# Values of a unit as four 128x128 products instead of sixteen 64x64 ones, and layer 1 of each expert on fewer slots

## The chip, the cores and the metric

The kernel runs on one core of one Trainium2 chip. The time is that of one execution on the device in microseconds (us), and kernels are compared by the medians of several runs. Engines: TensorE (PE in the profile; PEld is its weight load), VectorE (DVE), ScalarE (ACT), GpSimd (POOL) and SyncE (SP), which issues DMA transfers, as POOL and ACT also do.

## The reference

Linear attention with a norm, then a mixture of experts with one expert per token; only tokens with a positive skip score are computed.

```python
# q, k, v: (8, 8, 576, 64)
kv  = np.einsum('bhsd,bhse->bhde', k, v)              # a 64x64 state per batch and head
out = np.einsum('bhsd,bhde->bhse', q, kv)
rms = np.sqrt(np.mean(out * out, axis=-1, keepdims=True) + 1e-06)
out = out / rms * g_norm
x   = out.transpose(0, 2, 1, 3).reshape(4608, 512)
# experts: w_gate (512, 8), w1 (8, 512, 1024), w2 (8, 1024, 512)
do_compute = x @ w_skip > 0
xc = x[do_compute]                                    # other rows of x pass unchanged
e_idx  = np.argmax(xc @ w_gate, axis=1)
gate_w = softmax(xc @ w_gate)[chosen expert]
for e in range(8):
    mask = e_idx == e
    y[mask] = gate_w[mask] * (np.maximum(xc[mask] @ w1[e], 0) @ w2[e])
out[do_compute] = xc + y
```

## The kernel before, in words

Everything is in fp32 on PE. The order of the instructions on each engine is written out by hand: what the program issues first runs first on that engine.

**Attention.** Eight batches with eight heads each; the heads are taken as two groups u of four, and the four are indexed by w and a. For each batch `state` forms k-transposed times v in three thirds of 24 64x64 products each (`sum_ps`, line 336). `state_t` transposes the result (347), `state_m` multiplies it by the gate and skip weights (358), so that each head's state gets 9 more columns on either end for the router's logits, and `state_s` moves a copy to the other half of the partitions (366). After each of these ScalarE copies the result from PSUM into the batch's tile `kvd` (342, 350, 360, 369). There are five such tiles, and before the change each holds two versions of the state: index 0 as formed, index 1 with the partition halves exchanged.

The queries go in 36 units of 256 tokens by four heads: four units per batch (32 "ordinary" units, two token halves i by two head groups u), and after each four batches two units for the tokens left over (`x8`, i is None). A loop over n issues for each unit:

- `turn(n + 1)`: the next unit's queries are transposed by four PE transposes (403), and ScalarE copies them to `qT` (406);
- `values(n)`: `qT` times the state, 73 columns per head (443), into a PSUM tile of two banks, of which there are two; ScalarE squares them (449). For i = 0 `turn_8` also transposes left-over queries (422);
- `norm(n - 1)`: VectorE multiplies the previous unit by its inverse root mean square (474), with `squares` (457) and `root` (464) ahead of it; GpSimd adds the logits (491 to 497) and multiplies by the norm's weight into `xb` (507), and each batch's `xb` is stored;
- parts of the next batches' state, one third or one of `state_t`, `state_m`, `state_s` at a step: batch b's six parts stand at steps n-6 to n-1 ahead of its first unit n;
- loads of k and v three batches ahead and of q two ahead, on SyncE's queue, with stores of `xb` between them.

Beside this run the ranking of the experts and the slot numbers (VectorE, in groups at n = 12, 22 and at the end). When the second group is ranked, the weights of the first expert are loaded, behind which later stores of `xb` queue.

**Experts.** Experts are taken in order of their token counts, r = 0 to 7. Each has `CAPS[r]` slots; tokens over that would go through a loop of further rounds (line 1316). The slots are cut into pieces of 128, 64 and 32 (`plan_of`), and each piece's rows are gathered from `out` by an indirect DMA on GpSimd's queue (925), transposed (935) and copied to `xt`. For r = 0 both layers are direct products (`layer_1`, `layer_2`). From r = 1 on, `fast_1` forms layer 1 by Strassen's scheme, seven block products in place of eight, with half of the slots, `end // 2`, as the moving width (1033), sums on VectorE (975, 981, 1037) and copies on ScalarE (1043); it is 56 products of that width per expert. `fast_2` does the same for layer 2's first two pieces, and the rest of the pieces are direct products (965). In `fast_1` the next expert's tokens are transposed near the end, which needs their gathers. `result` (1166) adds the gated output to the gathered rows on VectorE and scatters them to `out` on GpSimd's queue (1175); the gathers of the next expert but one stand behind these scatters.

The widths of layer 1 and the pieces both follow from `CAPS`:

```python
    CAPS = (352, 352, 320, 288, 288, 288, 256, 256)
...
                todo = pieces[r]
                end = todo[-1][0] + todo[-1][1]
```

Of the kernel before, what the change touches and what calls it, by code (L numbers as in the profile page):

```python
# [8 lines left out]
FP32 = mybir.dt.float32  # L9
# [3 lines left out]
ALU = mybir.AluOpType  # L13
# [4 lines left out]
def kernel(  # L18
# [43 lines left out]
    nc = tc.nc  # L62
# [16 lines left out]
    PK = 2 * KD  # L79

    KVD = 5
    CAPS = (352, 352, 320, 288, 288, 288, 256, 256)
    CK = CAP // 128
    NCOL = E * CK
    ROUNDS = N // CAP
# [170 lines left out]


    kinds = {}
    for r, cap in enumerate(CAPS):
        off = cap // P * P  # L260
        for m in (64, 32):
            if cap - off >= m:
                kinds.setdefault((off % P, m), []).append((r, off))
                off += m
        assert off == cap
# [21 lines left out]
    gate_k = keep.tile([P, NT, 3], BF16)  # L287

    srow = keep.tile([P, NCOL], FP32)
    nc.vector.memset(srow[:, :], 0.0)  # L290

    top = keep.tile([P, E], FP32)
    nc.vector.tensor_copy(out=top[:, :], in_=ebase[:, :])
# [17 lines left out]

    kvds = []
    for i in range(KVD):
        kvds.append(kvd_pool.tile([P, 2, 2, PK], FP32, name=f"kvd{i}"))

    sum_all = ps_kv.tile([P, 2, 512], FP32, name="sum_ps")
    sum_ps = sum_all[:, :, 0:2 * D].rearrange("p a (u d) -> p a u d", u=2)
    sw_ps = g_ps[:, 0:2 * PK]
    kvT_ps = g_ps[:, 0:2 * P].rearrange("p (u x) -> p u x", u=2)
    lg_ps = g_ps[:, 2 * PK:2 * PK + 4 * G].rearrange("p (u a g) -> p u a g", u=2, a=2)  # L320

    def ends_of(x):

# [4 lines left out]
    def state(b, third):  # L328

        kt, vt = kts[b], vts[b]  # L330
        for i in range(6 * third, 6 * third + 6):
            u, c = divmod(i, C)
            for w in range(2):
                for a in range(2):
                    r = slice(a * 64, (a + 1) * 64)
                    nc.tensor.matmul(  # L336
                        out=sum_ps[w * 64:(w + 1) * 64, a, u, :],
                        lhsT=kt[r, 2 * u + w, c, :], rhs=vt[r, 2 * u + w, c, :],
                        start=(c == 0), stop=(c == C - 1), skip_group_check=True)
        if third < 2:  # L340
            return
        nc.scalar.copy(
            out=kvds[b % KVD][:, 0, :, G:G + 2 * D].rearrange("p u (a d) -> p a u d", a=2), in_=sum_ps)

    def state_t(b):
        for u in range(2):
            nc.tensor.transpose(out=kvT_ps[:, u, :], in_=kvds[b % KVD][:, 0, u, G:G + 2 * D],
                                identity=ident[:, :])
        kvT = att_pool.tile([P, 2, P], FP32, tag="kvT", name="kvT", bufs=1)
        nc.scalar.copy(out=kvT[:, :, :], in_=kvT_ps)  # L350
        kvTs[b] = kvT

    def state_m(b):
        kvT = kvTs.pop(b)
        for u in range(2):
            for w in range(2):
                r = slice(w * 64, (w + 1) * 64)
                nc.tensor.matmul(out=lg_ps[r, u, :, :], lhsT=kvT[:, u, r], rhs=gw_b[:, u, :, w, :],
                                 start=True, stop=True, skip_group_check=True)
        nc.scalar.copy(out=ends_of(kvds[b % KVD][:, 0, :, :]), in_=lg_ps)  # L360

    def state_s(b):

        for w in range(2):
            r, o = slice(w * 64, (w + 1) * 64), slice((1 - w) * 64, (2 - w) * 64)
            nc.tensor.matmul(out=sw_ps[o, :], lhsT=ident[r, r],  # L366
                             rhs=kvds[b % KVD][r, 0, :, :].rearrange("p u k -> p (u k)"),
                             start=True, stop=True, skip_group_check=True)
        nc.scalar.copy(out=kvds[b % KVD][:, 1, :, :].rearrange("p u k -> p (u k)"), in_=sw_ps)


    units = []
# [54 lines left out]
    def values(n):  # L427
        _, b, i, u = units[n]
        qT = qTs.pop(n)

        ps = sum_all if n >= THIRD and (n - THIRD) % 3 == 0 else \
            ps_o.tile([P, 2, 512], FP32, tag="o", name="o_ps")

        done = turn_8(b, u, ps) if i == 0 else None
        for w in range(2):
            for a in range(2):
                cols = slice(a * KD, (a + 1) * KD)
                for hf in range(2):
                    for r in range(2):
                        rows, to = slice(r * 64, (r + 1) * 64), slice(hf * 64, (hf + 1) * 64)  # L440
                        kvd = kvds[(b if i is not None else 4 * b + 2 * hf + r) % KVD]
                        x, y = (a, hf) if i is not None else (hf, a)
                        nc.tensor.matmul(  # L443
                            out=ps[to, r, w * PK + a * KD:w * PK + (a + 1) * KD],
                            lhsT=qT[rows, w, x, y * 64:(y + 1) * 64],
                            rhs=kvd[rows, w ^ r, u, cols],
                            start=True, stop=True, skip_group_check=True)
        sq = att_pool.tile([P, 2, 2, 2 * D], FP32, tag="sq", name="sq", bufs=2)
        nc.scalar.activation(out=sq[:, :, :, :], in_=heads(ps, G, G + 2 * D), func=ACT.Square)  # L449
        if done:  # L450
            done()
        ops[n] = (ps, sq)
# [27 lines left out]
    def finish(n, xl):  # L480
# [12 lines left out]
        if u == 1:  # L493
            del halves[nq]
            nc.gpsimd.tensor_tensor(out=lp[:, 0, :, :, :], in0=lp[:, 0, :, :, :],
                                    in1=lp[:, 1, :, :, :], op=ALU.add)
            nc.gpsimd.tensor_tensor(out=lgs[g][:, t0:t0 + 2, :], in0=lp[:, 0, :, 0, :],
                                    in1=lp[:, 0, :, 1, :], op=ALU.add)
        if i is None:
            if u == 0:  # L500
                xbs[b, i] = xb_pool.tile([P, 2, DM], FP32, tag="x8", name="x8", bufs=1)
# [1 line left out]
        else:  # L503
# [2 lines left out]
            xb = xbs[b, 0][:, i, :, :]  # L506
        late.append(lambda: nc.gpsimd.tensor_tensor(  # L507
            out=xb[:, :, 4 * u * D:(4 * u + 4) * D].rearrange("p r (w x) -> p r w x", w=2),
            in0=xl[:, :, :, G:G + 2 * D],
            in1=g_b[:, :, :].rearrange("p a d -> p (a d)").unsqueeze(1).unsqueeze(1)  # L510
                .to_broadcast([P, 2, 2, 2 * D]), op=ALU.mult))
        if n == NU - 2:
# [316 lines left out]
    with tc.tile_pool(name="wpool_b", bufs=1, reuse_waits="tile") as wpool_b, \  # L829
# [69 lines left out]


        def plan_of(r):
            pieces = [(c * P, P, r * CK + c) for c in range(CAPS[r] // P)]
            i = 0
            for (_, m), rs in kinds.items():
                for j, (r_, off) in enumerate(rs):
                    if r_ == r:
                        pieces.append((off, m, i + j))
                i += len(rs)
            return pieces
# [34 lines left out]
        def new_xt():  # L944
            return ffn.tile([P, DC, CAP], FP32, tag="xt", name="xt")

        def new_ht():
            return ffn.tile([P, FC, CAP], FP32, tag="ht", name="ht")

        def layer_1(r, xt, ht, cols, fs):  # L950
            for f in fs:
# [241 lines left out]
                for piece in pieces[r]:  # L1193
                    gather_piece(xgs[r], piece, src, asrc)

        def experts(pieces, srcs, xt, ht, yps0, tables, group):

            for r in range(E):
                load_ahead(r)
                if r:  # L1200
                    gather_all(r + 1, pieces, *srcs)
                todo = pieces[r]
                end = todo[-1][0] + todo[-1][1]
                new = {}

                def enter(some):
# [16 lines left out]
                    fast_1(r, xt, ht, end // 2, w2_sums(r), lambda: enter(more[0:1]))  # L1223
                    enter(more[1:])
                if more:
                    n = (more[-1][0] + more[-1][1]) // 2
                    beside = x_sums(r + 1, new["xt"], n) + (w1_sums(r + 1) if r else [])
                if r == 0:
                    for piece in todo:
# [12 lines left out]
                del w_sb[r]  # L1242
                if more:
                    xt, ht = new["xt"], new_ht()

        def rounds():

# [24 lines left out]
        assert plan[0][0] == first  # L1272
        plan[0] = plan[0][1:]
        xt0, ht0 = new_xt(), new_ht()
        expert_in(xg0, xt0, first)
        drain(choose(LAST))
        bv = columns(0, NE, colid_i, row_k, 2, gat_pool, NE)
# [19 lines left out]
        def first_tables(layer, tables):  # L1297
# [8 lines left out]
            agate = slot_pool.tile([P, NRES], FP32, tag="agate", name="agate")  # L1306
            nc.vector.tensor_copy(out=agate[:, :], in_=again_of(gate))
            return (tables[0], gate), (tables[1], agate)
        experts(plan, (src, asrc), xt0, ht0, yps0, (rows, arows), "first")

        order.__exit__(None, None, None)

# [3 lines left out]
        with tc.For_i(1, n_rounds, 1):  # L1316
            nc.vector.tensor_single_scalar(out=colid[:, :], in_=colid[:, :], scalar=CK, op=ALU.add)
            nc.vector.tensor_single_scalar(out=number_f[:, :], in_=number_f[:, :],
                                           scalar=float(CAP), op=ALU.add)
            nc.vector.memset(srow[:, :], 0.0)  # L1320
            add_pieces(srow[:, :], place_all(colid, row_k, 2), 2)

            left = slot_pool.tile([P, NCOL], FP32, tag="left", name="left")
            nc.vector.tensor_tensor(
                out=left[:, :].rearrange("p (r c) -> p r c", c=CK),
                in0=number_f[:, :].unsqueeze(1).to_broadcast([P, E, CK]),
                in1=caps[:, :].unsqueeze(2).to_broadcast([P, E, CK]), op=ALU.is_ge)
            nc.vector.tensor_tensor(out=srow[:, :], in0=srow[:, :], in1=left[:, :], op=ALU.mult)
            rows, src = slot_rows(slice(0, NCOL), slot_pool, "")
            for r in range(2):  # L1330
                gather_all(r, whole, src, None)
            gate = slot_gates(colid)
            xt0 = new_xt()
            for piece in whole[0]:
                expert_in(xg0, xt0, piece)
            experts(whole, (src, None), xt0, new_ht(), None, ((rows, gate), None), "more")


# [26 lines left out]
```

## Time and profile before

| | |
|---|---|
| median of 3 runs | 428.54 us (427.44 to 429.47) |
| the profiled execution | 427.44 us |
| its span, first to last instruction | 425.5 us |
| granted PE clock, mean | 0.92 |
| PE busy | 364.6 us (86%), 4601 matmul records |
| VectorE / ScalarE / GpSimd busy | 249.8 / 135.5 / 118.9 us |
| moved by DMA | 81.79 MB, 192 GB/s on average |
| first unit's values end | 19.2 us |
| first tokens of the experts transposed | 143.3 us |
| passes r = 1 to 7 begin | 199.3, 234.3, 264.0, 293.6, 324.2, 354.0, about 387 us |

A line of the profile's list gives start, duration, engine, line of the kernel, operation, the tiles and shapes, and how many alike; in brackets is how long the engine had been idle before it, and what ended that. "issue" there means that the profile shows nothing that the engine waited for. PE's matmuls are pipelined, so their rate is read from start to start and not from a row's own duration. An fp32 matmul appears as two matmul records, each with its weight load; a PE transpose as one.

### The profile page before, as it was taken

To read this page: it belongs to the slowest core of one execution; us is meant where nothing else is said; L and a number is where in the kernel's file an instruction comes from. 1 tells how busy PE (TensorE), PEld (TensorE's weight loads), DVE (VectorE), ACT (ScalarE), POOL (GpSimd) and SP (SyncE) were. 2 spreads that over 40 slices of the span, in tenths; PEclk is the share of its full clock that TensorE was granted. 3 is DMA by queue.
4 is the path that set the end of the run, shared out by engine and by line. 5 is a ranking of instruction groups with operands and counts; after the bars stand their busy time and mean duration, and the time that the engine had idled before them with its cause. 6 is when DMAs were issued, how large, how long until landed. Compare 5 with 4: busy or idle time off the path is not lost.

```text
span 425.5 us, 11081 instructions
## 1 busy us (share of the span) xinstructions
PE 364.6 (86%) x4601; PEld 309.6 (73%) x4601; DVE 249.8 (59%) x619; ACT 135.5 (32%) x360; POOL 118.9 (28%) x184
## 2 busy tenths in 40 slices
PE   7868775957876597999999999999999999989970
PEld 4556554746755484966987997998988988979960
DVE  3123353865887775154674765766766776858620
ACT  1344463445354230120340350240430430422300
POOL 2033454663456807012201221121121203101010
PEclk9589898879696698899999999999999999999995
DMA  8999989594769597052740733743752672501000
GB/s 302 390 390 385 326 233 373 169 298 168 211 229 347 140 295 261 10 219 66 236 176 36 250 102 156 245 118 153 246 193 77 237 241 79 205 27 50 2 27 20
DMA packets 31293, 81.79 MB, mean 192 GB/s; under 512 B 1850, under 2 KB 1858, under 8 KB 31236
## 3 DMA queue, kind: packets, MB, share of 16 engines
q1 hardware_dynamic: 26688, 66.59, 45.8%
q0 software_dynamic: 4528, 14.41, 10.5%
q8 instruction: 38, 0.62, 0.6%
q14 instruction: 19, 0.16, 0.1%
q10 hardware_dynamic: 20, 0.02, 0.0%
HBM read 66.80 MB, written 14.48 MB: 191 GB/s over the span
## 4 chain that ended last, share of the span: by engine, by line
PE 67%; issue 12%; DMA 11%; DVE 3%; ACT 2%; POOL 2%; SPq 0%; DVEq 0%; POOLq 0%; ACTq 0%
PE bank L1033 37%; PE bank L965 7%; PE bank L954 6%; PE sum_ps L336 5%; PE o_ps L443 4%; DMA out_dram<-xb 4%; DMA v<-in_v_dram 3%; PE q_ps L403 3%; DMA xg<-out_dram,src 2%; PE bank L935 2%; DVE xl L474 2%; DMA k<-in_k_dram 1%; DMA xg<-out_dram,asrc 1%; PE g_ps L366 1%; ACT qT L406 1%
## 5 line engine op out<-in xcount | busy, mean ns | idle before, releaser
L1033 PE MATMUL bank<-xt,w 128*128 128x144 f32 (+3 forms) x336 | 56.5, 291 | 0.3 <-DVE bank L1037 0.3
L1043 ACT COPY p<-bank 128x144 f32<-128x144 f32 (+4 forms) x70 | 20.9, 299 | 105.8 <-PE bank L1033 91.7
L1033 PEld LDWEIGHTS bank<-xt,w 128*128 128x128 f32 x336 | 47.8, 190 | 2.2 <-DVE bank L1037 1.5
L1037 DVE TENSOR_TENSOR bank<-bank,p 128x144 f32<-128x144 f32 (+4 forms) x70 | 23.8, 340 | 39.6 <-PE bank L1033 37.5
L336 PE MATMUL sum_ps<-v,k 64*64 64x64 f32 x1152 | 29.6, 248 | 13.5 <-issue 11.5
L1175 POOL DMA_INDIRECT out_dram<-xg,rows x16 | 16.2, 1011 | 79.6 <-DVE xg L1172 79.0
L507 POOL TENSOR_TENSOR xb<-xl,g_b 128x512 f32<-128x512 f32 x32 | 38.1, 1191 | 1.0 <-DMA out_dram<-xb 0.8
L336 PEld LDWEIGHTS sum_ps<-v,k 64*64 64x64 f32 x1152 | 26.4, 160 | 15.9 <-issue 15.3
L1033 PE MATMUL bank<-xs,s 128*128 128x144 f32 (+3 forms) x224 | 37.4, 292 | 0.0
L965 PE MATMUL bank<-w,ht 128*32 128x128 f32 (+2 forms) x448 | 36.6, 322 | 0.0
L443 PE MATMUL o_ps<-kvd,qT 64*64 64x73 f32 x960 | 27.7, 252 | 10.3 <-issue 6.2
L443 PEld LDWEIGHTS o_ps<-kvd,qT 64*64 64x64 f32 x960 | 22.0, 152 | 17.8 <-issue 12.3
L457 DVE TENSOR_REDUCE rs<-sq 128x8 f32<-128x512 f32 x36 | 24.5, 679 | 15.5 <-ACT sq L449 15.5
L1033 PEld LDWEIGHTS bank<-xs,s 128*128 128x128 f32 x224 | 31.6, 190 | 1.0 <-ACT p L1043 0.3
L925 POOL DMA_INDIRECT xg<-out_dram,src x15 | 15.9, 1063 | 55.7 <-PE bank L1033 36.3
L1175 POOL DMA_INDIRECT out_dram<-xg,arows x8 | 9.0, 1129 | 78.1 <-DVE xg L1172 77.8
L965 PEld LDWEIGHTS bank<-w,ht 128*32 128x32 f32 (+2 forms) x448 | 20.4, 121 | 13.6 <-issue 10.9
L406 ACT COPY qT<-q_ps 128x512 f32<-128x512 f32 x32 | 18.8, 587 | 32.5 <-PE q_ps L403 32.3
L491 POOL TENSOR_TENSOR lp<-xl 128x36 f32<-128x36 f32 x36 | 9.2, 255 | 71.3 <-DVE xl L474 69.4
L471 DVE RECIPROCAL rs<-rs 128x8 f32<-128x8 f32 x36 | 7.2, 200 | 36.8 <-ACT rs L464 36.2
L474 DVE TENSOR_TENSOR xl<-o_ps,rs 128x584 f32<-128x584 f32 x33 | 25.3, 767 | 4.0
L1033 PE MATMUL bank<-w,ht 128*128 128x256 f32 x112 | 27.1, 385 | 0.0
(196 smaller groups left out, 709.3 us busy)
## 6 DMA issues: line engine op xcount, KB each, us to landing
w<-in_moe_w_dram SPq DMA_DIRECT2D x16, 2048.0 KB, 10.7
q<-in_q_dram SPq DMA_DIRECT2D x8, 1152.0 KB, 12.9
k<-in_k_dram SPq DMA_DIRECT2D x7, 1152.0 KB, 12.2
v<-in_v_dram SPq DMA_DIRECT2D x7, 1152.0 KB, 15.1
out_dram<-xb SPq DMA_DIRECT2D x8, 512.0 KB, 4.6
out_dram<-xb POOLq DMA_DIRECT2D x8, 512.0 KB, 7.3
k<-in_k_dram SPq DMA_DIRECT2D x2, 576.0 KB, 4.1
v<-in_v_dram SPq DMA_DIRECT2D x2, 576.0 KB, 7.4
```

The source lines that it names most:

```text
L336: nc.tensor.matmul(out=sum_ps[w * 64:(w + 1) * 64, a, u, :], lhsT=kt[r, 2 * u + w, c, :], rhs=vt[r, 2 * u + w, c, :], start=(c == 0), stop ...
L406: nc.scalar.copy(out=qT[:, :, :, :].rearrange("p w a t -> p (w a t)"), in_=ps[:, :, :, :, :].rearrange("p w a h t -> p (w a h t)"))
L443: nc.tensor.matmul(out=ps[to, r, w * PK + a * KD:w * PK + (a + 1) * KD], lhsT=qT[rows, w, x, y * 64:(y + 1) * 64], rhs=kvd[rows, w ^ r, u, ...
L457: nc.vector.tensor_reduce(out=rs[:, :, :], in_=sq[:, :, :, :].rearrange("p x y (a d) -> p x (y a) d", a=2), axis=AX.X, op=ALU.add)
L474: nc.vector.tensor_tensor(out=xl[:, :, :, :].rearrange("p x y (a k) -> p x (y a) k", a=2), in0=ps[:, :, 0:2 * PK].rearrange("p x (h k) -> ...
L507: late.append(lambda: nc.gpsimd.tensor_tensor(out=xb[:, :, 4 * u * D:(4 * u + 4) * D].rearrange("p r (w x) -> p r w x", w=2), in0=xl[:, :, ...
L954: nc.tensor.matmul(out=hps[:, cols], lhsT=w_sb[r][0][:, dc, f * P:(f + 1) * P], rhs=xt[:, dc, cols], start=(dc == 0), stop=(dc == DC - 1))
L965: nc.tensor.matmul(out=yps[q * m:(q + 1) * m, 0:n], lhsT=ht[:, f, off:off + m], rhs=w_sb[r][1][:, f, q * n:(q + 1) * n], start=(f == 0), s ...
L1033: nc.tensor.matmul(out=out, lhsT=lhsT(i), rhs=rhs(i), start=start and i == 0, stop=i == k - 1, skip_group_check=True)
L1037: nc.vector.tensor_tensor(out=to, in0=x, in1=y, op=ALU.add)
L1043: nc.scalar.copy(out=t, in_=x)
L1175: ins = nc.gpsimd.indirect_dma_start(out=cut_rows(m)[:, :], out_offset=bass.IndirectOffsetOnAxis(ap=rows[:, col:col + 1], axis=0), in_=x, ...
```

## The change

Two things change.

1. For ordinary units the state tile `kvd` gets a second index and twice the room: for each copy w and each half r of the partitions it holds the state in one block and zeros in the other. A unit's sixteen products of 64x64 by 73 columns become four products of 128x128 by two pieces of 73 columns, in which one weight tile covers two heads' rows and the zeros keep them apart. The results of a unit lie in another order in PSUM, and the readers follow. `state_t` becomes four matmuls against halves of the identity in place of two transposes, `state_m` two matmuls in place of four, and each of ScalarE's three copies into `kvd` becomes two on half of the partitions. At the start the zeros are written, two memsets per tile, those of the first tile on VectorE and the others on GpSimd. The left-over units keep 64x64 products.

2. `CAPS` is smaller: 344, 336, 320, 280, 272, 264, 256, 256. `ROOMS` rounds it up to multiples of 32, which gives the former capacities, and the pieces, gathers and layer 2 go by `ROOMS`. Layer 1 runs on `CAPS[r]` columns. The columns of `ht` between the two are set to zero by GpSimd (`blank`), and slots over the capacity get row numbers out of range from the initial value of `srow`, which takes three small VectorE operations in place of a memset.

```diff
-    CAPS = (352, 352, 320, 288, 288, 288, 256, 256)
+    CAPS = (344, 336, 320, 280, 272, 264, 256, 256)
+    ROOMS = tuple(-(-cap // 32) * 32 for cap in CAPS)
...
-    nc.vector.memset(srow[:, :], 0.0)
+    beyond = setup.tile([P, CK], FP32)
+    nc.vector.tensor_single_scalar(out=beyond[:, :], in_=number_f[:, :], scalar=float(CAP), op=ALU.add)
+    nc.vector.tensor_tensor(
+        out=srow[:, :].rearrange("p (r c) -> p r c", c=CK),
+        in0=beyond[:, :].unsqueeze(1).to_broadcast([P, E, CK]),
+        in1=caps[:, :].unsqueeze(2).to_broadcast([P, E, CK]), op=ALU.is_ge)
+    nc.vector.tensor_single_scalar(out=srow[:, :], in_=srow[:, :], scalar=float(RSPACE), op=ALU.mult)
...
-        kvds.append(kvd_pool.tile([P, 2, 2, PK], FP32, name=f"kvd{i}"))
+        t = kvd_pool.tile([P, 2, 2, 2, PK], FP32, name=f"kvd{i}")
+        for r in range(2):
+            (nc.vector if i < 1 else nc.gpsimd).memset(t[r * 64:(r + 1) * 64, :, :, 1 - r, :], 0.0)
+        kvds.append(t)
+
+    def own(b, w):
+
+        return kvds[b % KVD][w * 64:(w + 1) * 64, :, w, w, :]
...
-        nc.scalar.copy(
-            out=kvds[b % KVD][:, 0, :, G:G + 2 * D].rearrange("p u (a d) -> p a u d", a=2), in_=sum_ps)
+        for w in range(2):
+            nc.scalar.copy(out=own(b, w)[:, :, G:G + 2 * D].rearrange("p u (a d) -> p a u d", a=2),
+                           in_=sum_ps[w * 64:(w + 1) * 64, :, :, :])
 
     def state_t(b):
         for u in range(2):
-            nc.tensor.transpose(out=kvT_ps[:, u, :], in_=kvds[b % KVD][:, 0, u, G:G + 2 * D],
-                                identity=ident[:, :])
+            for w in range(2):
+                r = slice(w * 64, (w + 1) * 64)
+                nc.tensor.matmul(out=kvT_ps[:, u, r], lhsT=kvds[b % KVD][:, u, w, w, G:G + 2 * D],
+                                 rhs=ident[:, r], start=True, stop=True)
...
         for u in range(2):
-            for w in range(2):
-                r = slice(w * 64, (w + 1) * 64)
-                nc.tensor.matmul(out=lg_ps[r, u, :, :], lhsT=kvT[:, u, r], rhs=gw_b[:, u, :, w, :],
-                                 start=True, stop=True, skip_group_check=True)
-        nc.scalar.copy(out=ends_of(kvds[b % KVD][:, 0, :, :]), in_=lg_ps)
+            nc.tensor.matmul(out=lg_ps[:, u, :, :, :], lhsT=kvT[:, u, :], rhs=gw_b[:, u, :, :, :],
+                             start=True, stop=True)
+        for w in range(2):
+            nc.scalar.copy(out=ends_of(own(b, w)), in_=lg_ps[w * 64:(w + 1) * 64, :, :, w, :])
...
+                if i is not None:
+                    nc.tensor.matmul(
+                        out=ps[:, w, 0:2 * PK].rearrange("p (r k) -> p r k", r=2)[:, :, cols],
+                        lhsT=qT[:, w, a, :], rhs=kvds[b % KVD][:, u, w, :, cols],
+                        start=True, stop=True, skip_group_check=True)
+                    continue
                 for hf in range(2):
                     for r in range(2):
...
-            pieces = [(c * P, P, r * CK + c) for c in range(CAPS[r] // P)]
+            pieces = [(c * P, P, r * CK + c) for c in range(ROOMS[r] // P)]
...
+        def blank(ht, r):
+            if CAPS[r] < ROOMS[r]:
+                nc.gpsimd.memset(ht[:, :, CAPS[r]:ROOMS[r]], 0.0)
...
-                end = todo[-1][0] + todo[-1][1]
+                end = widths[r]
...
-                    n = (more[-1][0] + more[-1][1]) // 2
+                    n = widths[r + 1] // 2
...
                     xt, ht = new["xt"], new_ht()
+                    if yps0 is not None:
+                        blank(ht, r + 1)
```

## The prediction

> **What bounds the kernel now.** Times are us from the start of the profiled execution: 427.44 us, 1.9 of them outside its span of 425.5; the median of the runs is 428.54. I read the busy table by stages, then TensorE's (PE's) waits up to 127, then its timeline.
>
> ```profile
> 19.20:101.80 82.60, 58.05 (x1686) 47.37 (x1686) 40.53 (x82) 37.62 (x94) 37.94 (x67) 0.88 0.91 311
> 101.80:127.10 25.30, 21.03 (x569) 17.32 (x569) 20.43 (x48) 14.58 (x37) 13.28 (x24) 0.87 0.58 178
> 127.10:143.30 16.20, 7.64 (x193) 6.29 (x193) 12.32 (x28) 6.63 (x16) 11.36 (x20) 0.75 0.81 272
> ...
> 354.00:385.00 31.00, 29.50 (x191) 27.02 (x192) 22.65 (x54) 8.44 (x25) 5.26 (x5) 1.00 0.32 104
> ```
>
> Columns: length; busy time of PE, PE's weight loads, VectorE (DVE), ScalarE (ACT), GpSimd (POOL); clock; DMA share; GB/s. No engine is full before 143, and nothing but PE is full after 199.
>
> ```profile
> PE sum_ps L336 <- issue: 11.5, 6, 3.5
> PE o_ps L443 <- issue: 6.2, 5, 2.2
> PE g_ps L358 <- issue: 4.8, 1, 4.8
> PE o_ps L443 <- DVE xl L474: 3.1, 4, 1.8
> ...
> PE sum_ps L336 <- DMA v<-in_v_dram: 1.0, 1, 1.0
> ```
>
> PE mostly waits for nothing the profile shows ("issue"), hardly for data. One such stop, inside a product whose operands are ready:
>
> ```profile
> 54.93 0.34 PE L443 MATMUL o_ps<-kvd,qT 64*64 64x73 f32 x4
> ...
> 57.49 0.73 PE L443 MATMUL o_ps<-kvd,qT 64*64 64x73 f32 x28 [2.22 <-issue]
> ```
>
> Counting PE's records (a weight load and a matmul each count one; an fp32 matmul makes two of both), the stops come before numbers 696, 951, 1206, 1462, 1716, 1972, 2227, 2482: 256 apart but for a few lost records. Each ends 1.2 to 1.5 us after a 16 KB packet of queue q8 lands, and PE makes 9,202 records for q8's 38 packets:
>
> ```profile
> q8 instruction: 38, 0.62, 0.6%
> ```
>
> So PE runs out of instructions there. Releases are 5.9, 6.5, 6.2, 7.7 and 6.6 us apart (38.91 to 71.71), mean 6.6: a refill's round trip under the loads. There are 13 stops up to 127: 23.0 us, 21.55 of them before 101.8. The trace's clock record adds half-speed stretches after long gaps (26.1-29.5, 46.6-50.0, 70.5-77.3, 90.9-97.8), with 15.8 us of PE work; 32 value products take 0.67 us at full and 1.18 at half clock, so about 6.8 us is lost there. Work at full clock up to 101.8 is 58.05 - 6.8 = 51.3.
>
> **Part 1, values as four 128x128 products.** PE's price is start to start in dense rows:
>
> ```profile
> 206.01 0.76 PE L1033 MATMUL bank<-xs,s 128*128 128x176 f32 x4
> 206.61 0.76 PE L1033 MATMUL bank<-xt,s 128*128 128x176 f32 x4
> ...
> 278.42 0.65 PE L1033 MATMUL bank<-xt,s 128*128 128x144 f32 x4
> 278.91 0.65 PE L1033 MATMUL bank<-xt,w 128*128 128x144 f32 x4
> ```
>
> Four take 0.60 at 176 columns, 0.49 at 144: 149 and 123 ns each (112 at 128, and 111.5 at 3 columns: a floor). Eight at 146 columns: 1.00 us. Before, from the start of one group to the start of the next at full clock, the transposes of a unit take 0.58 (33.01 to 33.59) and its values 0.56 to 0.67 (52.73 to 53.29, 33.59 to 34.26), mean 0.62. After, the transposes take 0.49, as they do where another 128-row group follows (83.90 to 84.39), the values 1.00, and 0.05 more because a 64x64 group follows half of them: 1.54, +0.34 per ordinary unit. The moving operand lies in two pieces of 73; no row here has that. If it cost like 176 columns, the unit would take +0.53; I take the 144-column row, the nearer in width.
>
> The Trainium skill, TensorEngine Tiling (Array Packing), Theoretical Speedup, gives 64x64 tiles up to 4x where both dimensions are small, and so speaks against the change: by the full 4x, an estimate, a unit would go from 0.62 to 2.48 and 27 units would cost 50 us, where the rows above make it 27 x 0.34 = 9.
>
> In state_t two transposes (0.28 to 0.35 to the next group) become four matmuls, eight records at the floor, 0.89; in state_m 0.35 becomes four records, 0.45. Together +0.68 per batch. state_s issues what it did.
>
> Stage to 101.8 (19 ordinary units, 5 batches' state): +6.5 + 3.4 = +9.9 of PE work. Records fall from 3,383 by 19 x 48, plus 5 x 4, to 2,491: 9.7 refills, not 13.2. Work per refill rises from 51.3 / 13.2 = 3.9 us to 61.2 / 9.7 = 6.3, against a round trip of 6.6. The work is uneven: of a batch's four steps, three hold 96 records of state sums each and run at 5.7 us per 256 records, the one with state_t is far slower. Stops remain where the dense part meets a refill, so I take 0.8 us per refill: 8 us instead of 21.55, -13.5. Ends: 0 us (-21.5) and 1.65 each as now (16 left, -5.5). Clock: short stops leave it up, -5.5 (ends 0 and -6.8). Waits for xl (1.2 here): -1.0, since PE comes later. Sum -10.1.
>
> By the Trainium skill, Runtime: NRT & Kernel Launch, Instruction fetch mechanics, refills of 256 instructions are mostly hidden; then nothing would be saved and the part would cost its +9.9. The 256 agrees with the trace; "hidden" does not (23.0 us of stops).
>
> 101.8 to 127: one refill stop (1.42), VectorE 20.4 of 25.3 with the ranking. 8 x 0.34 + 2 x 0.68 = +4.1; stop -0.7; xl wait (1.82) -1.3; the wait for state_s's copy (0.99) +0.4, there being two copies: +2.5.
>
> Start (half clock): VectorE's three small operations for srow (+0.4) and two memsets of 64x584 (between 0.12, the 128x72 memset, and 0.77, the 584-wide multiply; 0.5 each) let state_t begin at 13.4, not 12.54: +0.85; state_t +1.15, state_m +0.34, values of unit 0 +0.75; 0.93 is covered by the wait for v at 20.1: +2.2. Ends +0.5 and +4.
>
> 127 to 143: the end hangs on POOL and on stores behind 4 MB of weights (POOL's multiply at 136.87 waits for one). Values grow 4 x 0.34 or twice that at half clock; PE's own waits there (0.49, 1.38) cover most: +0.7. Ends 0 and +3.
>
> What I cost at nothing: ScalarE gets three more copies per batch (0.38 + 0.19 + 0.40): 8 us in all. It is 46% busy to 101.8 and the copies stand a step ahead of their readers; if its qT copy came late for them, up to 0.8 per batch. POOL's eight memsets of kvd (0.6 each by its 64x512 row, 0.51) run at 2 to 7 us, where it is idle to 20; the store of zeros behind them has no reader before 134. SyncE's queue keeps its order, and no transfer is added.
>
> **Part 2, layer 1.** Pieces, gathers and layer 2 stay, since the rooms are the old capacities. The inputs give 339, 333, 318, 275, 270, 264, 255 and 211 tokens by rank, so no second round runs; one expert fills its 264 slots exactly, and a chip that counted one token more would run the loop (0.01, among the slower). Passes 1, 3, 4, 5 shrink by 8, 4, 8, 12 columns in 112 records, pass 0 by 8 in 64; at 0.83 ns a column: 0.75, 0.37, 0.75, 1.1, 0.43 = 3.4. Passes 3 to 5 then meet the gathers:
>
> ```profile
> 311.33 0.95 POOL L925 DMA_INDIRECT xg<-out_dram,asrc  x1 [0.30 <-issue]
> ...
> 314.71 0.30 PE L935 MATMUL bank<-ident,xg 128*128 128x128 f32 x1 [0.52 <-DMA xg<-out_dram,asrc]
> ...
> 340.63 0.97 POOL L925 DMA_INDIRECT xg<-out_dram,src  x1 [0.30 <-issue]
> ...
> 344.23 0.63 PE L935 MATMUL bank<-ident,xg 128*128 128x128 f32 x4
> ```
>
> Tokens arrive 3.4 to 3.7 us after issue: pass 4 waits already, passes 5 and 3 (issue 280.87, need 284.25) have no slack, and the gathers follow the earlier pass's stores, not layer 1. So passes 0 and 1 pay (the latter has 2 us of slack) and 0.1 of the rest: -1.3. Ends -3.4 (gathers move along) and 0 (140 priced as 144, 168 as 176). The blanks (five POOL memsets, about 0.25 each by its small adds) stand between stores and gathers, where POOL waits 6 to 8 us; without that cover they would delay each gather by 0.25.
>
> **Sum:** -10.1 + 2.5 + 2.2 + 0.7 - 1.3 = -6.0; 427.4 - 6.0 = 421.4, said as 421. My base lies 1.1 below the median, less than the 0.5% (2.1 us) that a measurement can tell from no change.
>
> **Rivals.** (a) Refills stay as costly: denser loads stretch the round trip, each of 9.7 stops keeps 1.65 us and the half clock stays. Then +9.9 - 5.5 + 4.1 + 2.2 + 0.7 - 1.3 = +10: 437. For it: DMA share is 0.91 in that stage and rises if it shortens. Against: more work per refill. It decides where 9.7 stops eat what is gained: 9.9 - 1.0 + 4.1 = 13.0 of added work against 21.55 - 9.7 s, so from s = 0.9 us, or 1.4 if the clock mends by 5.5.
> (b) Refills hide entirely, clock full: -21.5 - 6.8 + 9.9 - 1.0 = -19.4, rest +4: 412. For it: 6.3 against 6.6. Against: round trips up to 7.7, and one stop of 4.77.
> (c) Another pace setter (loads, VectorE's chain) keeps the stage at 82.6: +2.5 + 2.2 + 0.7 - 1.3 = +4: 431. For it: DMA 0.91. Against: after 21 PE never waits for a load, and VectorE is at 49%.
> (d) The slots change nothing in time, since every pass meets its gathers: 1.3 higher, 423; a variant of each case, as is the full 3.4 (419).
>
> **Numbers.** Forecast 0.52, (a) 0.15, (b) 0.20, (c) 0.13. Forecast alone: 415 to 428. The bounds of the unknown costs (values up to 0.19 x 27 = 5 more, the start, the refills between 0 and 16, the gathers) carry it to 411 and 433; that leaves out about 0.11 of (a) and 0.06 of (b). Faster by 0.5% (below 426.4): 0.45 of the forecast, (b), and 0.04 of (c): 0.69. Within: 0.06 + 0.06 = 0.12. Slower: the rest, 0.19.
>
> **What would show it.** Right: value rows of x8 at about 1.0 us; "issue" before 102 falls to about 8; clock near 1 in 20-100; unit 22's values at about 94; the transposes into xt wait 0.3 to 1 us in passes 3 to 5. Wrong: stops above 1.4 us per refill, eight value records at 1.2 us or more, new PE waits for ACT's kvd copies, or a load that PE waits for.

## The result: 743.91 us, a second round of all experts

The changed kernel takes 743.91 us (median of 4 runs, 741.94 to 746.34) where the kernel before takes 427.99 in the runs beside it: a ratio of 1.7389, 95% interval 1.7296 to 1.7482. The forecast was 421. In all that follows, medians are over all runs and ratios over those in the faster of two states in which an execution can fall, so the two can differ a little.

The profiled execution took 741.94 us, with a span of 740.2. Its busy table in two stretches, up to the values of unit 22 and after the first round's last full products (columns as in the prediction: length; busy time of PE, weight loads, VectorE, ScalarE, GpSimd; granted clock; DMA share; GB/s):

```profile
19.20:86.10 66.90, 62.90 (x1253) 56.31 (x1252) 42.30 (x82) 44.94 (x112) 37.39 (x67) 0.99 1.01 362
...
391.00:740.00 349.00, 323.04 (x1572) 260.16 (x1570) 166.67 (x376) 78.03 (x193) 51.41 (x50) 0.96 0.32 98
```

The second line is new as a whole: the kernel before ends at 425.5. PE is busy for 323 us of it, almost nine tenths of what it does in the whole kernel before (364.6). The timeline of GpSimd, VectorE and PE around 391 shows what it is:

```profile
391.56 0.98 POOL L1204 DMA_INDIRECT out_dram<-xg,rows  x1 [23.01 <-DVE xg L1201]
...
392.53 0.16 DVE L1350 TENSOR_SCALAR number_f<-number_f 128x3 f32<-128x3 f32 x1
392.64 0.08 DVE L1352 MEMSET srow<- 128x24 f32 x1
...
392.85 1.28 POOL L1204 DMA_INDIRECT out_dram<-xg,rows  x1 [0.30 <-DVE srow L1352]
...
401.16 2.01 POOL L950 DMA_INDIRECT xg<-out_dram,src  x1 [7.03 <-DVE src L729]
...
406.10 1.08 PE L960 MATMUL bank<-ident,xg 128*128 128x128 f32 x4 [2.51 <-DMA xg<-out_dram,src]
```

Lines 1350 and 1352 stand in the loop for left-over tokens, which the kernel before never entered. After the last stores of the first round it makes new row numbers, gathers again, and then works through all eight experts. PE's groups in that stretch, kept apart by shape, tell the size of each pass:

```profile
L994 PE MATMUL bank<-w,ht 128*128 128x512 f32 x160 | 71.1, 592 | 0.0
L1062 PE MATMUL bank<-xt,w 128*128 128x192 f32 x336 | 68.2, 328 | 0.0
L1062 PE MATMUL bank<-xs,s 128*128 128x192 f32 x224 | 45.0, 329 | 0.0
...
L983 PE MATMUL bank<-xt,w 128*128 128x384 f32 x64 | 23.6, 534 | 0.7 <-ACT xt L963 0.7
```

The products are 192 wide in seven passes (336 = 7 x 48) and 384 in the first: every expert runs on all 384 slots, whatever it has left. From one pass's first token transposes to the next's it is 38.7 us (513.04 to 551.74).

The line about the instruction queue, and what PE waited for from 19.2 to 110:

```profile
q8 instruction: 44, 0.72, 0.4%
```

```profile
PE o_ps L457 <- DVE xl L496: 1.4, 3, 0.7
PE o_ps L457 <- ACT kvd L386: 1.2, 2, 0.9
PE q_ps L421 <- issue: 0.8, 1, 0.8
PE o_ps L457 <- ACT kvd L357: 0.8, 1, 0.8
PE g_ps L364 <- POOL lp L517: 0.6, 1, 0.6
PE o_ps L440 <- DVE xl L496: 0.4, 1, 0.4
PE g_ps L599 <- issue: 0.3, 1, 0.3
PE sum_ps L350 <- issue: 0.2, 1, 0.2
```

Attention itself became faster than the forecast had it. The first two lines of the table in the prediction, which goes to 127, stood at 11.5 and 6.2 us of "issue"; now the largest such wait is 0.8, and all of them together are 1.3. Unit 22's values come at 86.09 (before 101.77, forecast 94), the first expert's tokens are transposed at 127.15 (before 143.30), and the first round's last store is issued at 392.85 (before 413.67). So two separate questions arise: why the loop ran, and why attention gained about 16 us, where the whole change was forecast to gain 6.

**Why the loop ran.** The tokens were counted per expert before the forecast, but put in order by their final counts. The kernel does not order them so: `rank_experts` is called when the second of three groups of tokens is counted (in `gating`, for g = LAST - 1), that is after 22 of 36 token tiles, 2816 of 4608 tokens. Worked out from the reference's inputs:

| rank in the kernel | 0 | 1 | 2 | 3 | 4 | 5 | 6 | 7 |
|---|---|---|---|---|---|---|---|---|
| tokens when ranked | 209 | 202 | 200 | 171 | 166 | 156 | 153 | 128 |
| tokens at the end | 333 | 339 | 318 | 264 | 275 | 270 | 255 | 211 |
| slots before | 352 | 352 | 320 | 288 | 288 | 288 | 256 | 256 |
| slots after | 344 | 336 | 320 | 280 | 272 | 264 | 256 | 256 |

Three experts are over by 3, 3 and 6 tokens. The old slots were equal (352, 352 and three times 288) wherever two experts come in the wrong order, and so covered both orders. The new ones descend strictly there.

### The profile page after: what moved, and what is told of

Its sections match the earlier page's. It is cut to its first block, busy times and chain, and to the rows that moved or that the text cites. A ratio compares the mean times of both kernels' runs of the same rounds, so it can differ in the third digit from the quotient of the medians.

```text
span 740.2 us, 13716 instructions
## 1 busy us (share of the span) xinstructions
PE 689.7 (93%) x5417; PEld 579.5 (78%) x5417; DVE 419.9 (57%) x997; ACT 222.2 (30%) x577; POOL 174.8 (24%) x245
## 4 chain that ended last, share of the span: by engine, by line
PE 61%; issue 17%; DMA 11%; DVE 4%; POOL 3%; ACT 2%; POOLq 0%; DVEq 0%; ACTq 0%
PE bank L1062 33%; PE bank L994 11%; PE bank L983 6%; DMA out_dram<-xg,rows 5%; DMA xg<-out_dram,src 3%; PE o_ps L457 2%; DMA out_dram<-xb 2%; PE bank L960 2%; PE sum_ps L350 2%; POOL out_dram L1204 1%; PE q_ps L421 1%; DVE xl L496 1%; POOL xg L950 1%; PE g_ps L364 1%; DMA xg<-out_dram,asrc 1%
## 5 line engine op out<-in xcount | busy, mean ns | idle before, releaser
L1062 PE MATMUL bank<-xt,w 128*128 128x192 f32 (+6 forms) x672 | 123.5, 308 | 0.3 <-DVE bank L1066 0.3
L1072 ACT COPY p<-bank 128x192 f32<-128x192 f32 (+7 forms) x140 | 43.8, 313 | 253.5 <-PE bank L1062 237.3
L994 PE MATMUL bank<-w,ht 128*32 128x128 f32 (+2 forms) x608 | 107.7, 393 | 0.0
L1062 PEld LDWEIGHTS bank<-xt,w 128*128 128x128 f32 x672 | 103.6, 190 | 4.2 <-DVE bank L1066 2.7
L1066 DVE TENSOR_TENSOR bank<-bank,p 128x192 f32<-128x192 f32 (+7 forms) x140 | 49.9, 357 | 90.3 <-PE bank L1062 88.6
L1062 PE MATMUL bank<-xs,s 128*128 128x192 f32 (+6 forms) x448 | 81.6, 308 | 0.0
L1062 PE MATMUL bank<-t,ht 128*128 128x256 f32 x224 | 53.5, 382 | 0.0
L1062 PE MATMUL bank<-t,hs 128*128 128x256 f32 x224 | 50.6, 379 | 0.0
L1062 PEld LDWEIGHTS bank<-w,ht 128*128 128x128 f32 x224 | 41.1, 190 | 9.3 <-issue 4.7
L983 PE MATMUL bank<-xt,w 128*128 128x128 f32 (+2 forms) x192 | 46.0, 406 | 2.1 <-ACT xt L963 1.6
L1062 PEld LDWEIGHTS bank<-t,hs 128*128 128x128 f32 x224 | 42.6, 190 | 5.8
L983 PEld LDWEIGHTS bank<-xt,w 128*128 128x128 f32 x192 | 34.8, 215 | 12.9 <-issue 2.4
```

The costliest lines, as they stand in the source:

```text
L983: nc.tensor.matmul(out=hps[:, cols], lhsT=w_sb[r][0][:, dc, f * P:(f + 1) * P], rhs=xt[:, dc, cols], start=(dc == 0), stop=(dc == DC - 1))
L994: nc.tensor.matmul(out=yps[q * m:(q + 1) * m, 0:n], lhsT=ht[:, f, off:off + m], rhs=w_sb[r][1][:, f, q * n:(q + 1) * n], start=(f == 0), s ...
L1062: nc.tensor.matmul(out=out, lhsT=lhsT(i), rhs=rhs(i), start=start and i == 0, stop=i == k - 1, skip_group_check=True)
L1066: nc.vector.tensor_tensor(out=to, in0=x, in1=y, op=ALU.add)
L1072: nc.scalar.copy(out=t, in_=x)
```

## The experiments

Two theories stand behind the runs: the loop is the whole loss and comes from the order of the slots, at a fixed price; and attention's gain is that of TensorE's instruction stops, which return with the number of records. The rivals are that the changed code costs or gains elsewhere. All ratios are to the kernel before in the same session.

**Slots in the kernel's own order.**

```diff
-    CAPS = (344, 336, 320, 280, 272, 264, 256, 256)
+    CAPS = (336, 344, 320, 272, 280, 272, 256, 256)
```

> The changed kernel with one line edited: the slots per expert in the order in which the kernel ranks the experts, 336, 344, 320, 272, 280, 272, 256, 256 for the 333, 339, 318, 264, 275, 270, 255 and 211 tokens that come in that order; rooms, blanks and all else stay. Theory (three experts of the changed kernel were given 3, 3 and 6 slots too few, and the loop for left-over tokens is the whole loss): the loop does not run; the first round of the changed kernel ended at 391.6 us where the old one's ended at 412.4, so the time is 428.0 - 20.8 = 407 us, range 404 to 411, with nothing behind the last scatter but the end. Rival (the new order of instructions or the new slots also cost something that the loop hides, or the loop is entered for another reason): over 420, or still about 744.

Measured: 407.93 us (406.59 to 414.59, 6 runs), before 426.82; ratio 0.9608, interval 0.9538 to 0.9679. One line of numbers takes 336 us off the changed kernel. A list fitted to the final counts in descending order could not have done this: 336 is less than 339, and 272 less than 275. So the order among experts is the one in the table. The page and PE's waits from 19.2 to 110 of this kernel:

```profile
span 404.8 us, 9626 instructions
...
q8 instruction: 32, 0.52, 0.5%
```

```profile
PE o_ps L457 <- DVE xl L496: 1.4, 3, 0.7
PE o_ps L457 <- ACT kvd L386: 1.2, 2, 0.9
PE q_ps L421 <- issue: 0.8, 1, 0.8
...
PE sum_ps L350 <- issue: 0.4, 1, 0.4
```

32 instruction packets are left of 38 (the changed kernel's 44 include the loop's), and 1.2 us of stops for nothing visible, of some 21.

**The values part alone.**

```diff
-    CAPS = (344, 336, 320, 280, 272, 264, 256, 256)
+    CAPS = (352, 352, 320, 288, 288, 288, 256, 256)
```

> The values part alone: the changed kernel with the old slots 352, 352, 320, 288, 288, 288, 256, 256, which are also their rooms, so that layer 1 is as wide as before and nothing is blanked. Theory (the values part alone shortens attention by 16 us, since TensorE's stops for instructions vanish): 428.0 - 16.2, and up to 3 less for the stage behind it, which starts at a warmer clock: 409 to 412 us, and 1 to 3.4 above the fitted slots. Rival (part of the gain before 127 us belongs to the slots): over 415.

Measured: 408.83 us (407.59 to 411.55, 6 runs), ratio 0.9638, interval 0.9571 to 0.9705. The gain is that of the values part. Its first expert transposes stood at 129.9 in the profiled execution. Against the fitted slots it is 0.9 us slower, just under what was expected and less than the runs can tell.

**The slots part alone**, in the kernel before:

```diff
-    CAPS = (352, 352, 320, 288, 288, 288, 256, 256)
+    CAPS = (336, 344, 320, 272, 280, 272, 256, 256)
+    ROOMS = tuple(-(-cap // 32) * 32 for cap in CAPS)
...
-                end = todo[-1][0] + todo[-1][1]
+                end = widths[r]
```

(and the rest of the change's second part: `blank`, `srow`, pieces by `ROOMS`).

> The slots part alone: the kernel before, its 64x64 values kept, with slots 336, 344, 320, 272, 280, 272, 256, 256 parted from rooms of 352, 352, 320, 288, 288, 288, 256, 256. Theory (only passes 0 and 1 pay, the others then wait for their gathers): -1.3 for 8 columns less in passes 0 and 1 each, and 0.1 for the rest, so 426.7 us; ends 424.6 (all passes pay) and 428.0 (none does). The transposes into xt of passes 3 to 5 wait 0.3 to 1 us for their gathers. Rival (the blanks or the later stores of the zeros delay something): above 428.5.

Measured: 424.19 us (423.37 to 427.51, 6 runs) against 426.82, ratio 1.0008, interval 0.9938 to 1.0078. By the runs the slots part can't be told from nothing. The traces say more, if one takes the times between the first transposes into `xt` of one pass and the next, fitted slots against the values part alone. Where pass 0, after its first piece, has 16 slots less, 15.93 against 16.79 us; pass 1 with 8 slots less, 29.86 against 30.20; pass 2, unchanged, 35.38 against 35.39; from pass 3 to pass 7, with 16, 8 and 16 less, 120.83 against 121.60 (in the kernel before 121.93, in this run 121.69). Two us in all: passes 0 and 1 pay in full, and of the 1.9 us of work that passes 3 to 5 lose (20 columns of moving width, 112 records, 0.83 ns) 0.2 to 0.8 arrives. The last figure is no more than a hint: the kernel with the even slots (below) loses only 1.1 us of work there and takes 120.58. For pass 0 it agrees, 16.36 us with 8 slots less.

**All values as 64x64 products again**, on the new layout of `kvd`, with the new state steps and the fitted slots:

```diff
-                if i is not None:
+                if wide:
                     nc.tensor.matmul(
                         out=ps[:, w, 0:2 * PK].rearrange("p (r k) -> p r k", r=2)[:, :, cols],
...
+                        kvd = kvds[(b if i is not None else 4 * b + 2 * hf + r) % KVD]
+                        x, y = (a, hf) if i is not None else (hf, a)
                         nc.tensor.matmul(
                             out=ps[to, r, w * PK + a * KD:w * PK + (a + 1) * KD],
-                            lhsT=qT[rows, w, hf, a * 64:(a + 1) * 64],
-                            rhs=kvds[(4 * b + 2 * hf + r) % KVD][rows, u, w, r, cols],
+                            lhsT=qT[rows, w, x, y * 64:(y + 1) * 64],
+                            rhs=kvd[rows, u, w, r, cols],
```

with `wide` false for every unit. It was run in two sessions.

> The fitted slots of the first run, and every unit's values as sixteen 64x64 products again, on the new layout of kvd and with the new state steps (so TensorE makes 48 records per ordinary unit more, and about 11 us less of matmul work by 0.34 us for each of 32 units). Theory (the gain is that of records: fewer instructions per work, so that the refills hide): the stops for instructions come back, some 23 us of them up to the end of attention, and the half clock with them; 428.0 - 1.3 for the slots, and 2 to 5 for the new state steps: 427 to 432 us. Rival (the gain comes from something else in the change, the layout of kvd or the copies): the time falls with the matmul work, 396 to 410 us.

> The kernel with all values as 64x64 products on the new layout once more, beside the two others on one chip. Theory (stops for instructions): 422 to 430 us, with over 15 us of stops without a visible cause up to 110 us, 256 records apart. Rival (the layout): 396 to 410 us.

Measured: 426.98 us (419.82 to 431.25, 4 runs; ratio 0.9936, interval 0.9806 to 1.0066), then 430.54 (428.60 to 432.90, 4 runs; ratio 1.0107, interval 1.0068 to 1.0147). The gain is gone, though PE has less matmul work, 11 us at full clock by the forecast's 0.34 a unit. Layout and copies are therefore not its cause. PE's waits from 19.2 to 110, and the instruction queue, of the second session's profile:

```profile
PE sum_ps L350 <- issue: 5.2, 3, 2.1
PE q_ps L421 <- issue: 3.3, 1, 3.3
PE g_ps L606 <- issue: 2.7, 1, 2.7
...
PE o_ps L468 <- issue: 1.7, 1, 1.7
```

```profile
q8 instruction: 38, 0.62, 0.6%
```

The stops are back: 12.9 us, less than the 15 expected, and 18.8 in the first session's profile. All six come before PE records 696, 950, 1714, 1970, 2988 and 3500, which lie 254, 764, 256, 1018 and 512 apart: once, three, once, four and two times about 255, as in the kernel before (256 but for lost records). With them comes the half clock: its stretches between 23 and 150 us make 52 us here, 38.3 in the first session, 13.7 with the wide products and 41 in the kernel before. It grows with the 64x64 products, though not in step with the stops: the two sessions' profiles of this one kernel have 12.9 us of stops with 52 of half clock and 18.8 with 38.3, and reach the experts at 150.0 and 150.2. How much each of the two costs by itself was not shown.

**Half of the units**: the same kernel with `wide` for the second unit of each pair only.

```diff
+        wide = i is not None and u == 1
```

> As the run with all values in 64x64 products, but only for the first of each pair of units (16 of 32 ordinary units); the other 16 stay as four 128x128 products. Theory (records per work against the time of a refill): the middle dose; records up to the end of attention lie halfway, so the work per 256 records is about 5 us against a round trip of 6.6 us, and some of the stops come back, 0.5 to 1.2 us per refill: 412 to 422 us. Rival (the gain is one of matmul shape or of waits on other engines, in proportion to units): within 1 us of the fitted slots with all units wide, or faster by the 5 us of matmul work saved.

Measured: 416.9 us (412.54 to 420.9, 4 runs), before 427.14. PE's waits from 19.2 to 110, and a stop between two groups in its timeline:

```profile
PE sum_ps L350 <- issue: 5.7, 5, 1.9
PE q_ps L421 <- issue: 4.6, 2, 2.7
...
PE o_ps L468 <- issue: 0.5, 1, 0.5
```

```profile
80.45 0.88 PE L350 MATMUL sum_ps<-v,k 64*64 64x64 f32 x48
84.04 1.11 PE L421 MATMUL q_ps<-ident,q 128*128 128x128 f32 x4 [2.71 <-issue]
```

10.8 us of stops, 35 instruction packets, 20.5 us of half clock, and the first expert transposes at 135.0. The doses side by side, each from its profiled execution (stops: the "issue" lines of PE's waits from 19.2 to 110, as far as the table lists them):

| values | q8 packets | stops, us | half clock 23 to 150, us | first expert transposes | median, us |
|---|---|---|---|---|---|
| all 64x64, old layout (before) | 38 | 21.6 | 41.0 | 143.3 | 426.8 to 428.5 |
| all 64x64, new layout, first session | 38 | 18.8 | 38.3 | 150.2 | 426.98 |
| all 64x64, new layout, second session | 38 | 12.9 | 52.1 | 150.0 | 430.54 |
| half and half | 35 | 10.8 | 20.5 | 135.0 | 416.9 |
| all 128x128, fitted slots | 32 | 1.2 | 13.7 | 127.2 | 407.93 |

By the same reading the other profiles with all values in 64x64 products have 16.6 us of stops (the loop in the kernel before, below) and 17.5 (the slots part alone); those with all in 128x128 products have 1.2 to 4.0. So the three doses keep apart, but a single execution does not fix the amount.

On the new layout the first 16 units made wide bring 10 to 14 us by the medians (426.98 and 430.54 to 416.9) and the other 16 bring 9. The four runs of the half dose lie in two pairs, though, near 413 and near 421, and by the lower pair the other 16 bring only 5: how the gain divides is open. That each half gains, while PE's work grows with each, is not.

**Three tokens over instead of twelve**, the fitted slots but for one:

```diff
-    CAPS = (336, 344, 320, 272, 280, 272, 256, 256)
+    CAPS = (336, 336, 320, 272, 280, 272, 256, 256)
```

> The fitted slots but for one expert: 336 instead of 344 for the expert that has 339 tokens, so that 3 tokens of one expert are left over instead of 12 of three. Theory (any left-over token starts one round of the loop, and the round has a fixed size: all eight experts on 384 slots each): the time is that of the changed kernel, 744 us, give or take 4. Rival (the cost follows the tokens left over): 407 + 336 x 3/12 = 491 us; or follows the experts over: 407 + 336/3 = 519 us.

Measured: 748.39 us (2 runs, 746.14 and 750.63), ratio 1.7547, interval 1.7344 to 1.7751. A quarter of the tokens costs the same round, within some 5 us.

**The loop in the kernel before**, by one number:

```diff
-    CAPS = (352, 352, 320, 288, 288, 288, 256, 256)
+    CAPS = (352, 320, 320, 288, 288, 288, 256, 256)
```

> The kernel before with one number edited: 320 slots instead of 352 for the second expert in rank order, which has 339 tokens, so that 19 are left over; values, slots and rooms otherwise as before. Theory (the round is as dear in the kernel before, nothing of the change makes it so): pass 1 is 32 slots narrower, about 3 us of layer 1 and 2 of layer 2, and then one round of about 336 us: 428 - 5 + 336 = 759 us, range 750 to 768. Rival (the changed code makes the round dear, the new zeros and blanks or the wider kvd): well under 740.

Measured: 754.74 us (2 runs, 754.34 and 755.14), ratio 1.7696, interval 1.75 to 1.7893. The old kernel pays the same. The busy tables of the two runs from just before the first round's last stores to the end, first the three tokens of the changed kernel, then the nineteen of the old one:

```profile
400.00:748.00 348.00, 322.75 (x1570) 259.90 (x1568) 166.42 (x375) 78.07 (x193) 51.39 (x50) 0.96 0.32 98
```

```profile
405.00:752.00 347.00, 321.97 (x1570) 259.64 (x1568) 166.39 (x375) 78.04 (x193) 51.38 (x50) 0.96 0.32 99
```

1570 matmul records and 322 us of PE in both, as in the changed kernel (1572 and 323.04): the price depends neither on how many tokens are left nor on the change.

**Slots that don't depend on the order among neighbours.**

```diff
-    CAPS = (344, 336, 320, 280, 272, 264, 256, 256)
+    CAPS = (344, 344, 320, 280, 280, 280, 256, 256)
```

> The changed kernel with slots that do not depend on the order among experts with close counts: 344, 344, 320, 280, 280, 280, 256, 256 (all counts of neighbours fit either way round). Against the slots fitted to the order, pass 0 is 8 columns wider and passes 3 and 5 are 8 wider; only pass 0 pays, by 0.4 us. Theory: the time of the fitted slots, 408 us, give or take 2, and as far below the kernel before. Rival (every column of layer 1 costs 0.09 us): 410.

Measured: 410.42 us (406.24 to 413.46, 6 runs), ratio 0.9572, interval 0.9524 to 0.9621, where the fitted slots had 0.9608 (0.9538 to 0.9679) in their session: the same within what the runs tell. Both beat the two kernels that were given. This list is the safer for these inputs; other inputs can still overrun it.

**Layer 1 of passes 3 to 5 on 224 columns**, with the fitted slots (the hidden values of slots above 224 are left out):

```diff
+    WIDE1 = CAPS[0:3] + (224, 224, 224) + CAPS[6:8]
...
-        experts(plan, CAPS, (src, asrc), xt0, ht0, yps0, (rows, arows), "first")
+        experts(plan, WIDE1, (src, asrc), xt0, ht0, yps0, (rows, arows), "first")
```

> The fitted slots, but layer 1 of passes 3, 4 and 5 computed on 224 columns instead of 272, 280 and 272 (the columns above are blanked, so the hidden values of the experts' last tokens are left out; pieces, gathers, layer 2 and stores are whole). The work taken away is 48 + 56 + 48 columns in 112 records at 0.83 ns, 14.1 us. Theory (the gathers hold these passes, and follow the stores of the pass before the last): TensorE's wait for the gathers grows by most of it, and the time falls by 0 to 4 us only: 404 to 408. Rival (the gathers move along with the shorter passes): the time falls by 10 to 14 us, 394 to 398.

Measured: 410.78 us (407.26 to 411.69, 4 runs), ratio 0.9598, interval 0.9556 to 0.9641, beside 410.42 with the even slots in the same session. Neither theory's number, and the run can't tell them apart, because the 14.1 us were worked out wrongly. The moving width is half the slots, and there is a floor. In PE's timeline of pass 4, fitted slots first, then this kernel:

```profile
280.97 0.64 PE L1062 MATMUL bank<-xs,s 128*128 128x140 f32 x4
281.45 0.64 PE L1062 MATMUL bank<-xt,s 128*128 128x140 f32 x4
```

```profile
286.18 0.61 PE L1063 MATMUL bank<-xs,s 128*128 128x112 f32 x4
286.63 0.61 PE L1063 MATMUL bank<-xt,s 128*128 128x112 f32 x4
```

Four take 0.48 us at 140 columns and 0.45 at 112: 112 records save about 0.8 us a pass, and less at 136, some 2 us in all. Of these the trace shows little: from pass 3 to pass 7 it takes 120.58 us against the fitted slots' 120.83, and PE's waits for gathers in that stretch are 2.5 us against 1.7. That fits gathers that hold these passes, but the even slots take 120.58 too and the changed kernel 119.94, with far less work taken away, so the stretch does not follow the slots within what single executions tell. Whether gathers or columns hold passes 3 to 5 was not shown by an experiment. Taking the gathers' wait for the earlier stores away was not tried: the waits stand between accesses to one tensor in memory, and nothing else in the kernel keeps those apart.

## Why the prediction was wrong, step by step

- **The step that failed: "The inputs give 339, 333, 318, 275, 270, 264, 255 and 211 tokens by rank, so no second round runs".** The counts are right; the ranks are not. The kernel ranks on 2816 of 4608 tokens, and the table above shows the ranks crossed twice, 333 ahead of 339 and 264 ahead of 275 and 270. Fitted to the kernel's order, the same code takes 407.93; so the loop is all of the loss, 336 us, and outweighs the roughly 20 us that the rest of the change gains. The forecast did see that an overrun would run the loop, and gave it 0.01, for one miscounted token. It priced neither the loop nor the code that orders the experts, and no rival named the crossing.
- **The stops.** The forecast kept 0.8 us for each of 9.7 refills, 8 us; 1.3 remained in the changed kernel. Work per refill was well placed, 62.90 us over 9.7 refills being 6.5 against the 6.3 forecast and the round trip of 6.6. What was wrong was the reading that uneven work would still meet a stop at each refill: with the mean work just under the round trip, nearly all stops went. The end of the range, 0 us, was much nearer. This is rival (b), "refills hide entirely, clock full", with 412; with the fitted slots, without the loop, it is the case that came true, at 408.
- **The clock.** Taken as -5.5, end -6.8; the clock to 86.10 is 0.99, so the end.
- **The work that was added.** PE was to have 61.2 us of work up to unit 22's values and is busy for 62.90 of the 66.90 us to there. The eight value records were put at 1.00 us, and at 1.05 with the change of shape; from the start of one such group to the next group they take 1.01 to 1.20, median 1.10. The transposes (0.49) and state_m (0.45, measured 0.46) were right, state_t's 0.89 measured 0.84.
- **The rule weighed against the change.** The Trainium skill, TensorEngine Tiling (Array Packing), Theoretical Speedup, gives up to 2x for a dimension of at most 64; the 4x for both dimensions is worked out from that, an estimate. The rows give 0.62 for sixteen of them against 1.10 for the four wide products, a factor of 1.8, and the runs give the wide ones the shorter time.
- **"Mostly hidden".** The Trainium skill, Runtime: NRT & Kernel Launch, Instruction fetch mechanics, says so of refills of 256 instructions. With the wide products the traces agree (1.2 to 4.0 us of stops); with 64x64 products they don't (12.9 to 21.6).
- **From unit 22 on.** +2.5 and +0.7 were forecast up to the first expert; it took 41.1 us (86.09 to 127.15) where it had taken 41.5, so nothing was lost there. The start came out a little better than the +2.2 forecast: the first unit's values begin at 20.54 against 17.93, +2.6, but the work behind them at 21.71 against 20.14, +1.6.
- **ScalarE's copies at no cost.** Wrong by 0.6 us up to unit 22: PE waits 0.8 for the copy at L357 and 0.3 for the one at L386, where the kernel before waits 0.5 for such a copy. The other 0.9 at L386 comes at 109.50; it is the wait that the forecast had counted (1.0 before, +0.4 forecast).
- **Layer 1.** -1.3, ends -3.4 and 0; the traces of the fitted slots give about -2, the runs -0.9. That passes 3 to 5 meet their gathers is visible: in pass 5 of the changed kernel the transposes wait as foreseen,

```profile
323.13 0.63 PE L960 MATMUL bank<-ident,xg 128*128 128x128 f32 x4 [0.36 <-DMA xg<-out_dram,src]
...
324.60 0.63 PE L960 MATMUL bank<-ident,xg 128*128 128x128 f32 x4 [0.39 <-DMA xg<-out_dram,src]
```

and pass 4's wait 0.17 and 0.49; pass 3's don't. The blanks are hidden: 0.23 and 0.30 us on GpSimd at 282.13 and 312.17, 7 us ahead of the gathers.

## What to carry to other kernels

A capacity that is cut close must be compared with the count of the very item that the program will put there, so read the code that sets the order and when it runs; and price the path that an overrun takes before giving it a small chance, here about 330 to 340 us for 3 tokens as for 12 or 19. Where PE stops for nothing that the profile shows, at equal distances in its records, compare the work per block of instructions with the time from one refill to the next: where the first is much the smaller (here 3.9 us against 6.6), fewer and larger products can win even though they cost more PE time. Here nearly all stops had gone at 6.5 against 6.6; where exactly the gain ends was not shown.

## What the runs showed of the hardware that was not expected

- Nearly all stops went although the mean work per refill, 6.5 us, stayed just under the 6.6 of the kernel before, and although it comes unevenly. Counted in records, allowing for the lost ones, blocks of 256 pass in 6.2, 6.0, 9.2, 5.6, 9.9, 5.5, 6.2 and 4.8 us in the changed kernel (22.05 to 75.34), with stops of 0.2 and 0.3 us in all of them; in the kernel before in 6.1, 6.4, 6.3, 5.9, 6.5, 6.2, 7.7 and 6.6 (20.11 to 71.72), with a stop of 1.0 to 3.5 us at each. So the 6.6 is not a floor under every block; what lets the dense ones pass without a stop was not shown.
- Six profiled executions whose attention is the same code (only the slots differ) transpose the first expert's tokens at 127.15 to 130.72 us. They differ by up to 3 us in their stops, and in the end of the half clock at the start: at 20.7 us in the changed kernel, at 22.8 with the even slots. A difference of 3 us between single executions need not come from an edit.
- Four fp32 products take 0.48 us at 140 columns, 0.45 at 128 (389.52 to 389.97 in the kernel before) and 0.45 at 112: narrowing from 128 to 112 saved nothing.
